# A fused attention and feed-forward kernel, its 1,400 operations put in another order up to the last stage

## The chip, the cores and the metric

The kernel runs on one core of a Trainium2 chip. The metric is the device time of one execution in microseconds (us), as the median of three runs. A core has TensorE (PE, matmuls), VectorE (DVE), ScalarE (ACT), GpSimd (POOL) and SyncE (SP). Each engine works through its own instructions strictly in order, and DMA transfers are issued from queues of POOL and SP.

## The reference, cut to what matters

```python
# q, k, v: (8, 12, 448, 64) float32
scores = (1 / sqrt(64)) * matmul(q, k.transpose(0, 1, 3, 2))
attn   = maximum(scores, 0) ** 2 / 448
x      = matmul(attn, v).transpose(0, 2, 1, 3).reshape(3584, 768)
h      = x @ w_in                                  # (768, 2048)
g      = 0.5 * h * (1 + erf(h / sqrt(2)))          # exact gelu
out    = g @ w_out                                 # (2048, 768) -> (3584, 768) float32
```

There is no softmax: the scores go through relu and a square, so each block of keys can be worked off by itself.

## The kernel before

**Tiling.** The work goes by batch (8), by group of four heads (3 groups, g0 to g2) and by block of 64 keys (7 blocks). Matmul operands are bf16.

**Into transposed form.** QK needs q and k with the head dimension on the partitions. Batches 0 and 1 are transposed on PE (`add_tk`, L607, for k; `add_tq`, L635, for q) and copied out of PSUM by DVE (L513) or ACT (L515). Batch 0 is worked in two halves of its 224 queries, so that the first half can begin when half of q is there. From batch 2 on, nine DMA transposes per batch on SP's queue do this (`add_T_dma`, L662): for each group one for k, one for its even and one for its odd q slots. The third kind reaches into the next group's q, so it waits for that load too.

**Attention.** QK (L736) writes score blocks into one of three double banks of PSUM ("w"). A relu takes them out, on ACT (L748) or on DVE (L750). A square on DVE (L757) makes the weights in place; there are 14 such buffers. AV (L797) sums a group over its blocks into a "w" bank, and a copy (L513 or L515) puts it into xT, two heads to 128 partitions.

**Feed-forward.** When all three groups of a half or of a batch are in xT, the first matmuls follow (`add_f1`, L849), 128 of the 2048 hidden columns at a time: `psh`, in one of two other PSUM banks ("f"), which the transposes of batches 0 and 1 use as well. ACT does the gelu (L859). Batch 0's first three tiles of hidden columns are computed by half rows (operations 141, 143 and 145 for the first half), so that PE has work before the second half of the queries is done; the first whole-row `psh` is operation 251. The second matmuls (`pso`, L1166) follow by groups of 256 rows; their sums and output copies are on DVE and ACT (L1147, L1200), three `osb` buffers hold results, and SP issues the stores (L1127; operations 386, 389, 435, 436 are the first). The last batches use sums over blocks of weights (L993, L1030, L1039, L1103) to save multiplications.

**Loads.** POOL's queue issues them: k (L548), q (L469), v (L566), `w_in` in five parts of three transfers (L486 to L488) and `w_out` in three (L492). Only the first group of batch 0 is loaded from other queues (L1312 to L1315). One buffer each holds the untransposed q and k of the DMA-transposed batches in turn, so before the loads of the next batch POOL runs a small copy, the "gate" (L703), that waits for the transposes of a group.

**Before the first data.** 45 matmuls on zeros (the "spin", L1333) run on PE. Later, "fills" (`add_fill`, L1493 to L1505) do the same in an "f" bank: a word Z1056 in the order is a fill of 1056 columns, in matmuls of at most 512 (L1499).

**What sets the order.** All operations are put in one list with their numbers. A constant, `ORDER` (L83 to L165), is a list of words that is written out in the code, each a letter for the engine (P for PE, A for ACT, D for DVE, G for POOL, S for SP, Z for a fill on PE) and an operation's number. `place` goes through it and gives each engine its instructions in that order:

```python
for word in ORDER.split():
    if word[0] == "Z":
        op, eng = next(fills), "PE"
    else:
        op, eng = self.open[int(word[1:])], names[word[0]]
    _, dur, lat = next(e for e in op.engines if e[0] == eng)
    ...
    self.commit(max(self.ready(op), free), op, eng, dur, lat)
```

So the list also says whether DVE or ACT does a relu or a copy. The waits between engines come from the operations' operands and buffers, not from the list.

The numbers that the text needs (b is the batch, g the group):

| operations | what they are |
|---|---|
| 0, 3 and 1, 4 | loads of k and of q's first half, b0 g1 and g2 |
| 2, 5, 6 | loads of v, b0 g0, g1, g2 |
| 7; 8, 9; 120, 124, 128 | load of q's second half, b0; `w_in` parts 0, 1; 2, 3, 4 |
| 117, 121, 125; 118, 122, 126; 119, 123, 127 | loads of b1: k, q, v of g0, g1, g2 |
| 147, 150, 153; 148, 151, 154; 149, 152, 155 | loads of b2: k, q, v |
| 228 to 236 | b2's transposes: k, even q, odd q of g0 (228, 229, 230), g1 (231 to 233), g2 (234 to 236) |
| 237, 240, 242; 238, 239, 241 | gates after b2's transposes; loads of `w_out` |
| 269 to 275; 398 to 406 | loads of b3; its transposes |
| 407, 410, 413; 408 to 416 without these; 541 to 549 | gates after b3's transposes; loads of b4; its transposes |
| 288, 306, 330; 440; 600, 624 | first QK in the list before: of b2 g0, g1, g2; of b3; of b4 g0 and g1 |
| 1435 | the identity matrix for PE's transposes (L1321) |

Of the kernel before, what the change touches and what calls it, by code (L numbers as in the profile page):

```python
# [80 lines left out]


ORDER = """  # L83
G0 G1 G2 G3 G1435 G4 G5 G6 A10 P11 D13 A16 P17 G7 D12 P14 D18 P42 P39 G8 P19 A15 P21 D43 P33 P36 D44
A40 D20 Z128 A22 P54 G9 P25 P23 A37 D34 P51 D26 P48 A55 Z1056 D35 A24 P69 D56 Z1024 D41 A49
P57 Z992 D38 A52 P63 Z448 G117 D70 P45 A58 D53 P66 A64 D50 P27 A46 G118 P31 D59 P60 D28 A67
G119 D32 A47 P78 P29 D65 G120 A61 P81 Z1088 D68 D30 A79 P93 D62 P108 Z544 D71 A82 P84 Z992
G121 A94 P75 D109 P72 G122 D83 A85 P90 P129 D80 G123 D73 A76 P105 A74 P102 D95 G124 P131 D130
A91 P141 D86 A106 D77 P111 P96 D132 A103 P165 P143 D92 A112 D104 D107 A97 P156 D113 P87 G125
D98 A166 P99 D110 G126 D88 A157 P114 A142 D100 A89 P174 G127 A101 P168 D115 P133 A144 P135  # L90
A116 G128 D175 P171 P159 A169 D134 P251 D136 D170 A160 P145 D158 A172 D167 A252 P162 P186 D176
P192 P243 A146 D161 G147 D173 A187 G148 P253 D193 A163 A244 D164 P195 G149 P180 P198 P137 A254
G150 P139 D196 A181 P183 P177 G151 D138 A199 D140 A184 P189 P219 P245 D178 G152 A190 D185 P247
G153 D194 A220 D179 A246 G154 P213 D188 P222 P204 P263 D221 A248 G155 D197 A214 D200 P265 D191
A205 D182 A264 P261 A223 A266 P216 D224 S231 P207 P201 D206 A262 A208 S229 P210 P259 D209 A217
D215 S232 P255 D211 A260 P249 D212 D218 A256 D202 P225 A203 S228 A250 P257 S230 A226 P267 D227
A258 P348 S234 A268 P350 S233 A349 P352 G237 A351 G238 P354 S235 A353 G239 P288 S236 P294 P282
P358 A355 G240 G241 D289 P356 D283 A359 P360 D295 A357 D290 P306 P279 P276 D296 P362 A361 D307
P364 D280 A363 P366 D277 A365 P368 A367 P370 A369 P300 P285 P291 G242 P372 A371 G269 D286 A292
P374 G270 D284 A373 G271 P318 P303 D301 P312 G272 P376 D308 A375 G273 A304 D319 P378 D278 A377  # L100
P380 D313 A379 D293 G274 D314 D390 P382 D305 G275 D302 A381 D391 D287 D281 P330 P309 P297 S398
D392 A331 D320 P315 S399 P384 D393 A298 D396 A310 S401 A383 D417 P387 D394 D419 A385 D311 A299
D395 A316 D317 P324 P321 D418 A325 P333 D397 P327 A388 P421 D420 D322 S400 A328 D323 P423 D326
A334 D422 S386 P339 P336 P342 P425 D424 D329 A343 D335 P427 S402 A426 D337 P429 G407 A340 G408
S403 D428 P431 G409 D344 D338 S389 D341 P440 P437 D332 P345 S404 D430 A438 P443 D441 P446 S405
P433 D432 A346 D347 A444 P509 A447 D434 P511 D439 G410 D448 S406 A510 G411 P449 D442 P452 G412
P455 P513 D562 A512 S435 D445 S436 A453 P515 D454 A450 A514 P517 D456 D451 P464 D457 P461 P458
S541 A465 P467 D462 A518 P470 G413 S542 P519 A516 G414 A459 G415 P521 D471 S543 G416 D472 A520
P523 D466 A468 D460 S544 A522 P479 D560 P476 P473 D469 P525 A524 D463 A477 P527 D480 A474 D478
A526 P529 D475 D481 A528 P488 P485 P482 S545 A489 P494 D486 A530 P491 P531 D487 D483 P533 D495  # L110
A532 S546 P535 D496 A484 D561 A492 P503 D490 P500 A534 P497 D493 P537 A536 G550 G551 S547 P564
D498 G552 A538 D504 S548 P539 D499 A501 G553 A565 D505 P600 G554 D502 P603 P506 G555 S549 A601
P606 D604 A540 P609 P566 D563 A507 D602 P568 D607 D567 P570 D610 A569 A508 P572 D571 P624 P612
P618 S704 P574 D580 D608 A613 D573 P576 S705 G556 A619 D581 G557 D582 P627 S706 D575 P615 G558
P584 D614 G559 D577 S578 A616 D611 P586 S707 D605 A628 D617 A625 P636 D620 P630 S579 A585 P621
D629 G713 A631 D637 P633 G714 P588 D587 S708 G715 A622 D626 D623 A634 P639 P642 P648 D583 P590
D638 A640 D635 A589 D632 P592 D641 A643 D591 P651 A649 S709 D644 P657 P645 D593 A652 P666 D658
P654 P594 D653 A646 D659 A655 D650 P596 A647 D667 S710 D595 P660 P766 P663 P672 D597 A661 D767
P674 A664 S711 D662 A673 D656 P676 D668 A675 D665 P772 P769 P669 S712 G716 D773 A770 P763 S598
P775 A677 G717 P678 S599 D670 G718 A764 D771 P680 G719 D723 A776 S867 D768 A679 P790 P778 D765  # L120
A671 P781 G720 P682 A681 D777 G721 D791 P684 G722 S868 D725 A683 P686 D779 A782 A685 P688 D783
D780 D774 P787 P793 P784 D724 S869 A788 P799 D794 A687 P796 P690 A689 D795 D789 A797 P692 D798
A691 P694 A693 P696 A785 A695 S870 P698 A786 A800 P802 P811 A697 P805 D801 P700 A699 A803 D812
P702 S871 D792 A806 D804 P814 P817 D807 P808 A815 S872 P823 D818 A701 P820 P727 G876 D816 A703
G877 D809 S873 A821 G878 D726 P729 A810 D819 A728 D822 P826 D813 A824 P829 S874 P906 P731 D730
G879 A830 G880 D827 S875 P733 G881 A907 D828 D831 P912 D825 P921 P832 D745 A913 P909 A732 D922
P924 P735 D734 A833 A925 P737 A910 D743 A834 P936 D914 P918 P933 D736 P739 D738 S741 D744 A934
P747 D908 G882 A937 D740 G883 P749 D938 A919 S978 G884 D935 A748 G885 D926 P942 P930 S742 P915
P751 D750 A931 D943 S979 P753 D920 A916 A752 D746 P755 D923 S980 D911 D944 P948 P945 D917 P927
D888 A949 D754 P939 P757 D950 A928 D886 D756 P759 A946 D887 A940 D758 A929 P835 D932 D947 D941  # L130
S981 P957 P954 P951 A836 D958 A955 P960 P963 D760 P837 D959 A961 D952 P839 D956 A953 S982 A838
P966 D964 P972 P969 D962 P841 A840 S983 D889 A973 D965 P843 S984 A842 D967 P847 A970 S985 A844
P845 D971 D968 S761 D974 P990 P987 D1067 P975 S986 A991 P993 D988 A846 P996 S762 P849 D992
A848 D1068 A976 D1070 P851 A997 D989 A850 P853 A994 A977 D995 P1005 P1002 A852 P999 P855 A854
D1006 A1003 P859 D1004 A1000 D998 A856 P857 D1007 D1001 P1011 P1014 P1008 D1059 A858 A1012
P1017 D1015 P1026 P861 A1009 D1063 A860 P863 D1060 A1018 D1010 P1020 A1027 P1029 D1061 P1023
A862 P865 D1016 A864 D1019 P890 A1021 D1028 D1022 A866 P892 D1062 A1024 A891 D1013 P894 D1025
A1030 D1069 D893 P1035 D1031 P1038 P1032 D1064 A895 A1036 D1066 P1041 D1037 A1039 P1044 P896
D1033 A1042 D1034 D1040 P898 A1045 D1043 D897 P1047 D1046 P1050 P1053 P900 D899 A1048 D1139
P902 D1049 A1051 D1140 A1054 P1071 D1052 D1055 P1056 D901 S904 A1072 D903 S905 P1088 D1141  # L140
P1073 D1057 P1090 A1089 D1058 P1143 D1074 D1091 P1075 D1065 P1092 A1144 P1077 D1142 A1076
D1179 P1094 A1093 D1180 P1079 D1078 P1096 D1095 P1145 D1080 D1097 A1081 P1082 D1181 A1098
P1099 D1146 P1085 D1083 P1102 D1100 A1084 P1105 D1086 A1101 P1122 D1103 A1087 P1107 D1182
A1106 P1124 A1123 P1147 A1104 D1108 D1125 P1109 P1126 A1148 P1111 A1110 P1128 A1127 P1113
D1112 P1130 D1129 P1149 D1114 D1131 A1115 P1116 A1132 P1133 D1150 P1119 D1117 P1136 D1134
A1118 P1151 D1120 A1135 D1137 A1121 P1153 D1291 A1138 D1292 D1152 P1155 D1159 D1154 S1157
P1163 D1160 D1156 S1158 P1165 D1161 D1164 P1167 D1162 D1166 D1293 P1169 D1294 A1168 P1171
D1170 P1173 D1253 D1172 P1175 D1251 D1174 S1177 P1183 D1252 P1200 D1176 S1178 P1185 A1184
D1254 P1202 A1201 P1255 D1186 D1203 P1187 P1204 A1256 P1189 A1188 P1206 A1205 P1191 D1190
P1208 D1207 P1257 D1192 D1209 A1193 P1194 A1210 P1211 D1258 P1197 D1195 P1214 D1212 A1196  # L150
P1217 D1198 A1213 P1234 D1215 A1199 P1219 A1218 P1236 A1235 P1259 A1216 D1220 D1237 P1221
P1238 A1260 P1223 A1222 P1240 A1239 P1225 D1224 P1242 D1241 P1261 D1226 D1243 A1227 P1228
A1244 P1245 D1262 P1231 D1229 P1248 D1246 A1230 P1263 D1232 A1247 D1249 A1233 P1265 A1250
D1264 P1267 D1271 D1266 S1269 P1275 D1272 D1268 S1270 P1277 D1273 D1276 P1279 D1274 D1278
P1281 D1280 P1283 D1282 P1285 D1365 D1284 P1287 D1363 D1286 S1289 P1295 D1364 P1312 D1288
S1290 P1297 A1296 D1366 P1314 A1313 P1367 D1298 D1315 P1299 P1316 A1368 P1301 A1300 P1318
A1317 P1303 D1302 P1320 D1319 P1369 D1304 D1321 A1305 P1306 A1322 P1323 D1370 P1309 D1307
P1326 D1324 A1308 P1329 D1310 A1325 P1346 D1327 A1311 P1331 A1330 P1348 A1347 P1371 A1328
D1332 D1349 P1333 P1350 A1372 P1335 A1334 P1352 A1351 P1337 D1336 P1354 D1353 P1373 D1338
D1355 A1339 P1340 A1356 P1357 D1374 P1343 D1341 P1360 D1358 A1342 P1375 D1344 A1359 D1361  # L160
A1345 P1377 A1362 D1376 P1379 D1383 D1378 S1381 P1387 D1384 D1380 S1382 P1389 D1385 D1388
P1391 D1386 D1390 P1393 D1392 P1395 D1394 P1397 D1405 D1396 P1399 D1403 D1398 S1401 P1407
D1404 D1400 S1402 P1409 D1406 D1408 P1411 D1410 P1413 D1412 S1423 P1415 D1414 P1417 D1416
P1419 D1418 S1424 P1420 D1421 S1425 D1422 S1426
"""  # L165


# [1368 lines left out]
```

## Time and profile before

| | |
|---|---|
| median of 3 runs | 370.13 us (369.83 to 370.37) |
| the profiled execution: its span (the page gives no other time of it) | 367.9 us, 8474 instructions |
| busy: PE, DVE, ACT, POOL | 359.3, 285.1, 199.4, 62.9 us |
| share of the span | 98%, 78%, 54%, 17% |
| read from memory, written to it | 45.61 MB, 11.01 MB |

How to read it: the span goes from the first to the last recorded instruction of one profiled execution, and is 2.2 us below the median of the runs. Busy times are sums over an engine's instructions; an engine can be busy and do nothing useful, as PE is with spin and fills. The view by stretches of time cuts the span into pieces and gives for each the busy time of every engine, the granted clock of PE and the share of the DMA engines. The view in order of time lists single instructions with start, length and, in brackets, the wait just before and what ended it; an entry "SPq" or "POOLq" is the issue of a DMA on that engine's queue, which takes time on the queue and lands later.

### The profile page before, as it was taken

What the parts mean: (1) busy time and instruction counts of PE and PEld (TensorE: products, weight loads), DVE (VectorE), ACT (ScalarE), POOL (GpSimd) and SP (SyncE); (2) the same over time, 40 slices, a digit from 0 to 9 for tenths busy, and PEclk for the clock granted to TensorE, in tenths of its full rate; (3) what the DMA queues carried; (4) which work ended last, traced back from release to release, by engine and by line L of the source; (5) the groups of instructions that cost most, each with busy time, mean ns of one, the idle gap of its engine ahead of it and who ended that gap; (6) DMA issues with size and microseconds to landing.
All of it is one profiled execution on the core that took longest, in us unless ns stands there. A gap on an engine that the chain in (4) does not pass through costs nothing.

```text
span 367.9 us, 8474 instructions
## 1 busy us (share of the span) xinstructions
PE 359.3 (98%) x3573; PEld 222.5 (60%) x3573; DVE 285.1 (78%) x473; ACT 199.4 (54%) x319; POOL 62.9 (17%) x103
## 2 busy tenths in 40 slices
PE   7999999999999999999999999999999999999995
PEld 6675654455544455544555544557876897688663
DVE  4998854699788889989598997998788558665862
ACT  5998954536367546765777568863540353045200
POOL 8766304230112140240302000000000000000000
PEclk9999999999999999999999999999999999999998
DMA  9999999999999999999999980002002301210233
GB/s 180 191 202 204 201 178 167 196 201 178 162 218 214 154 186 193 237 214 154 166 110 131 215 183 2 2 2 86 3 0 87 88 0 52 86 37 2 86 87 86
DMA packets 89542, 47.27 MB, mean 128 GB/s; under 512 B 55329, under 2 KB 86049, under 8 KB 89505
## 3 DMA queue, kind: packets, MB, share of 16 engines
q0 software_dynamic: 32912, 22.47, 43.8%
q1 hardware_dynamic: 55952, 23.76, 34.9%
q8 instruction: 28, 0.46, 0.5%
q10 hardware_dynamic: 640, 0.51, 0.4%
q14 instruction: 10, 0.07, 0.1%
HBM read 45.61 MB, written 11.01 MB: 154 GB/s over the span
## 4 chain that ended last, share of the span: by engine, by line
PE 78%; DMA 8%; SPq 5%; DVE 5%; issue 1%; POOL 1%; ACT 1%; DVEq 0%; POOLq 0%; ACTq 0%
PE pso L1166 30%; PE psh L849 19%; PE pb L993 13%; PE ps L736 8%; PE pav L797 7%; SPq L662 5%; DMA wout_sb<-in_moe_w_out_dram 4%; DVE a_sq L757 2%; DMA nq<-in_q_dram 1%; DVE t_sb L1103 1%; DMA qT<-nq 1%; DMA out_dram<-osb 1%; ACT a_sq L748 1%; PE tp L635 1%; DVE part L1030 1%
## 5 line engine op out<-in xcount | busy, mean ns | idle before, releaser
L748 ACT ACTIVATE a_sq<-ps 128x896 bf16<-128x896 f32 (+1 forms) x119 | 104.3, 918 | 36.8 <-PE ps L736 36.6
L757 DVE TENSOR_TENSOR a_sq<-a_sq 128x896 bf16<-128x896 bf16 (+1 forms) x169 | 97.0, 617 | 9.4 <-ACT a_sq L748 8.8
L849 PE MATMUL psh<-xT,win_sb 128*128 128x448 bf16 (+1 forms) x516 | 96.4, 340 | 0.4 <-issue 0.4
L849 PEld LDWEIGHTS <-win_sb 128*128 128x128 bf16 x516 | 48.1, 98 | 45.8 <-issue 9.7
L750 DVE TENSOR_SCALAR a_sq<-ps 128x896 bf16<-128x896 f32 (+1 forms) x50 | 53.5, 1078 | 17.1 <-PE ps L736 17.0
L859 ACT ACTIVATE h_sb<-psh 128x448 bf16<-128x448 f32 x80 | 43.2, 548 | 29.9 <-PE psh L849 29.6
L1166 PEld LDWEIGHTS <-s_sb 128*128 128x128 bf16 x424 | 40.7, 98 | 26.6 <-issue 2.0
L1030 DVE TENSOR_TENSOR part<-pb,part 128x448 f32<-128x448 f32 x60 | 34.6, 620 | 21.5 <-PE pb L993 21.5
L736 PE MATMUL ps<-qT,kT 64*64 64x448 bf16 (+1 forms) x756 | 47.9, 336 | 0.5 <-ACT a_sq L748 0.2
L1166 PEld LDWEIGHTS <-h_sb 128*128 128x128 bf16 x312 | 29.6, 98 | 22.5 <-issue 4.4
L1166 PE MATMUL pso<-wout_sb,s_sb 128*128 128x384 bf16 (+2 forms) x216 | 38.1, 320 | 0.1
L1166 PE MATMUL pso<-wout_sb,h_sb 128*128 128x384 bf16 x208 | 38.1, 326 | 0.0
L1166 PE MATMUL pso<-t_sb,s_sb 128*128 128x384 bf16 x208 | 38.1, 326 | 0.0
L797 PE MATMUL pav<-a_sq,v_sb 64*64 64x448 bf16 (+1 forms) x756 | 36.5, 329 | 0.3 <-issue 0.2
L736 PEld LDWEIGHTS <-kT 64*64 64x64 bf16 x756 | 18.5, 105 | 22.9 <-issue 17.1
L1039 ACT ACTIVATE h_sb<-part 128x448 bf16<-128x448 f32 x36 | 20.1, 578 | 20.2 <-DVE part L1030 19.9
L1200 DVE TENSOR_TENSOR osb<-pso,p_sb 128x384 f32<-128x384 f32 x39 | 21.7, 556 | 11.0 <-PE pso L1166 6.7
L993 PEld LDWEIGHTS <-win_sb 128*128 128x128 bf16 x288 | 27.6, 98 | 2.3 <-issue 0.4
L797 PEld LDWEIGHTS <-v_sb 64*64 64x64 bf16 x756 | 21.2, 107 | 11.7 <-issue 1.3
L703 POOL COPY gate<-qT 128x16 bf16<-128x16 bf16 x15 | 3.7, 246 | 111.0 <-DMA qT<-nq 111.0
L993 PEld LDWEIGHTS <-ws 128*128 128x128 bf16 x216 | 20.7, 98 | 0.0
L1147 DVE TENSOR_TENSOR s_sb<-h_sb 128x1024 bf16<-128x1024 bf16 x26 | 17.8, 685 | 2.3 <-PE pso L1166 2.3
(61 smaller groups left out, 298.4 us busy)
## 6 DMA issues: line engine op xcount, KB each, us to landing
nk<-in_k_dram POOLq DMA_DIRECT2D x23, 224.0 KB, 5.6
nq<-in_q_dram POOLq DMA_DIRECT2D x21, 224.0 KB, 8.3
v_sb<-in_v_dram POOLq DMA_DIRECT2D x5, 672.0 KB, 13.9
out_dram<-osb SPq DMA_DIRECT2D x8, 336.0 KB, 2.9
v_sb<-in_v_dram POOLq DMA_DIRECT2D x9, 224.0 KB, 8.6
out_dram<-osb SPq DMA_DIRECT2D x7, 288.0 KB, 3.2
out_dram<-osb SPq DMA_DIRECT2D x8, 240.0 KB, 3.0
win_sb<-in_moe_w_in_dram POOLq DMA_DIRECT2D x8, 192.0 KB, 8.6
```

The source lines that it names most:

```text
L736: nc.tensor.matmul(ps[64 * j : 64 * j + 64, e, x * w : x * w + w], kT[r, g, i * 128 + 64 * j : i * 128 + 64 * j + 64], moving, start=True, ...
L748: A.activation(ar, ps, AF.Relu, scale=c_att)
L750: V.tensor_scalar(ar, ps, c_att, 0.0, op0=mybir.AluOpType.mult, op1=mybir.AluOpType.max,)
L757: V.tensor_mul(box["a2"][:, :, :used], ar, ar)
L797: nc.tensor.matmul(pav[0][o2 : o2 + 64, e, :w], vt[b][r, 2 * g + e, bass.ts(i, D)], box["a2"][r, y, o : o + w], start=(i == 0), stop=(i == ...
L849: nc.tensor.matmul(ph[:, x * n : x * n + n], win_sb[:, kd, bass.ts(m + x, 128)], xT[b][:, kd, c], start=(kd == 0), stop=(kd == KD - 1),)
L859: A.activation(h_ring()[:, m : m + nm, o + c.start : o + c.stop], box[0][:, :S].rearrange("p (x n) -> p x n", x=nm), AF.Gelu,)
L993: nc.tensor.matmul(bank[name][:, y, z * HS : z * HS + HS], w[:, k, bass.ts(mm, 128)], right()[:, k], start=first and k == 0 and z == 0, st ...
L1030: V.tensor_add(get(to), ps(name), get(other))
L1039: A.activation(h_ring()[:, m : m + 2, o + half[c].start : o + half[c].stop], src().rearrange("p (x n) -> p x n", x=2), AF.Gelu,)
L1166: nc.tensor.matmul(box[bank][:, n0:n1], left()[:, kf], right()[:, kf, n0:n1], start=bool(need) and kf == 0, stop=kf == K2 - 1, skip_group_ ...
L1200: V.tensor_add(out()[:, n0:n1], box[bank][:, n0:n1], other()[:, n0:n1])
```

## The change

Only `ORDER` changes: it is replaced from its second line to the middle of its last stage; the last 164 operations stand as before. All operations, their operands and their buffers are the same, but for the fills: seven of eight go (Z128, Z1024, Z992, Z448, Z1088, Z544, Z992), and Z1056 stays. With seven fewer, the identity's number is 1428 instead of 1435. Lines below the list shift by two.

The opening, to the first whole-row `psh` (P251):

```diff
-G0 G1 G2 G3 G1435 G4 G5 G6 A10 P11 D13 A16 P17 G7 D12 P14 D18 P42 P39 G8 P19 A15 P21 D43 P33 P36 D44
-A40 D20 Z128 A22 P54 G9 P25 P23 A37 D34 P51 D26 P48 A55 Z1056 D35 A24 P69 D56 Z1024 D41 A49
-P57 Z992 D38 A52 P63 Z448 G117 D70 P45 A58 D53 P66 A64 D50 P27 A46 G118 P31 D59 P60 D28 A67
-G119 D32 A47 P78 P29 D65 G120 A61 P81 Z1088 D68 D30 A79 P93 D62 P108 Z544 D71 A82 P84 Z992
-G121 A94 P75 D109 P72 G122 D83 A85 P90 P129 D80 G123 D73 A76 P105 A74 P102 D95 G124 P131 D130
-A91 P141 D86 A106 D77 P111 P96 D132 A103 P165 P143 D92 A112 D104 D107 A97 P156 D113 P87 G125
-D98 A166 P99 D110 G126 D88 A157 P114 A142 D100 A89 P174 G127 A101 P168 D115 P133 A144 P135
-A116 G128 D175 P171 P159 A169 D134 P251
...
+G0 G1 G3 G1428 G4 G7 G118 A10 P11 D13 G2 A16 P17 D12 P14 G117 D18 P42 P39 G5 P19 D15 P36 D43
+G121 P21 A40 P33 D20 G6 P23 D44 A37 D22 P54 G8 P51 D41 P25 A34 D24 Z1056 D26 A55 P63 P57 D35 A52
+P31 P66 D64 P27 A58 D32 P108 P48 D38 P29 A67 D28 P81 P131 A109 G9 D49 P69 P45 A82 D56 P111 D50
+A70 P78 A46 D68 D47 A112 P75 P102 D53 A79 D30 P84 G122 P133 D59 A103 P60 D71 A85 G120 D65 P72
+D132 A76 D113 P93 A61 P129 A73 D80 D62 P90 D74 G125 P96 A94 P105 D130 P141 A91 D83 D110 A97 P165
+G124 P171 D134 P143 A142 D86 D95 A106 P168 D77 P135 A166 G126 D104 P87 D107 A172 P114 D98 A169
+D92 A88 P99 A115 D136 A89 P159 D116 P195 P145 G119 D167 A160 G128 A100 D196 P156 A144 D101 P174
+P162 A146 P137 P251
...
```

The words of the two DMA queues, each in its order. POOL's, to batch 4's last load (559 is a load of batch 5's v):

```diff
-0 1 2 3 1435 4 5 6 7 8 9 117 118 119 120 121 122 123 124 125 126 127 128 147 148 149 150 151
-152 153 154 155 237 238 239 240 241 242 269 270 271 272 273 274 275 407 408 409 410 411 412
-413 414 415 416
+0 1 3 1428 4 7 118 2 117 5 121 6 8 9 122 120 125 124 126 119 128 148 147 154 127 151 150 123
+237 238 239 149 153 241 240 272 152 242 271 270 155 269 274 273 407 408 275 413 409 410 414
+415 416 412 559 411
```

SP's, to batch 4's transposes:

```diff
-231 229 232 228 230 234 233 235 236 398 399 401 400 386 402 403 389 404 405 406 435 436 541
-542 543 544 545 546 547 548 549
+229 228 230 232 233 231 236 235 234 402 400 399 398 403 405 401 404 386 406 541 543 548 542
+549 435 547 545 389 546 436 544
```

The first QK of a group stand earlier among PE's words: those of batch 2's group 0 stand behind 39.9 us of PE's other work instead of 52.8, added up from the durations in the trace before. DVE gets 19 more operations (489 for 470) and ACT 19 fewer (298 for 317): 36 relus go from ACT to DVE and 32 the other way, the rest are copies and output sums.

## The prediction

> **What bounds the kernel now.** I read the page first, then stretches of 10 us, then the rows of the first 30 us and of the two DMA queues.
>
> ```profile
> span 367.9 us, 8474 instructions
> ...
> PE 359.3 (98%) x3573; PEld 222.5 (60%) x3573; DVE 285.1 (78%) x473; ACT 199.4 (54%) x319; POOL 62.9 (17%) x103
> ...
> PEclk9999999999999999999999999999999999999998
> ```
>
> PE is the bound, at the full clock. What can be won is time in which PE does nothing useful, and the stretches say where that lies:
>
> ```profile
> 0.00:10.00 10.00, 7.52 (x136) 6.29 (x138) 3.92 (x10) 6.03 (x9) 8.90 (x17) 1.00 1.02 183
> 10.00:20.00 10.00, 9.57 (x227) 6.45 (x225) 9.84 (x19) 9.35 (x14) 7.36 (x11) 1.00 1.45 190
> 20.00:30.00 10.00, 9.96 (x245) 7.67 (x242) 9.09 (x19) 8.92 (x16) 6.02 (x10) 1.00 1.28 205
> 30.00:40.00 10.00, 9.62 (x135) 6.24 (x135) 8.20 (x14) 8.37 (x12) 5.39 (x10) 1.00 1.27 202
> ```
>
> The columns are the stretch, its length, then PE, PEld, DVE, ACT, POOL, clock, DMA share, GB/s. From 10 to 20 DVE (9.84) and ACT (9.35) are full; PE's 9.57 holds the zero fills. So in the opening PE waits for relus, squares and copies. After 30 us only small PE waits are left: 0.38 in 30 to 40, 0.53 in 96 to 104, 0.18 at 241, 0.07 at 271.
>
> ```profile
> 9.72 0.39 PE L635 MATMUL tp<-ident,nq 112*64 112x112 bf16 x8 [0.86 <-DMA nq<-in_q_dram]
> ...
> 10.16 0.39 DVE L513 COPY qT<-tp 128x448 bf16<-128x448 bf16 x1 [0.75 <-PE tp L635]
> ...
> 10.55 0.91 ACT L515 COPY kT<-tp 128x896 bf16<-128x896 bf16 x1 [0.56 <-PE tp L607]
> ...
> 10.84 0.61 PE L1499 MATMUL fill<-zero 64*64 64x512 bf16 x3
> ```
>
> Group 2's q lands at 9.68, behind a v; PE, DVE and ACT all wait for it.
>
> **The change, part by part.** The span is the profiled execution's own 367.9; the median of the runs is 370.13, 2.2 above it, and I take that 2.2 as unchanged.
>
> *Fills.* 13 of 16 zero matmuls go. They lie between 8.46 and 18.99 and fill waits, so alone they save nothing. They cover the clock: it stays 1.00 through the 0.86 gap, and the spin's matmuls go from 107 to 56 ns apart after 2.8 us of work. Without the fills I find no gap over 1 us, so I price them at 0; were the clock lost, PE's first 2.8 us of full rows would take twice as long, up to 1.4.
> [...]
>
> *k and q ahead of v.* Landings of before: k g1 6.02, q g1 6.66, v 7.76, k g2 9.05, q g2 9.68. Taking out the v (1.1) puts q g2 at 8.6. The v loads then land at about 12.5, 14.8 and 17.1 (from 7.76, 10.84 and 12.69), and the new order asks for them at 13.9, 17.6 and 18.4: hidden. win goes from 16.5 and 18.5 to 19.1 and 21.1 and is asked for at 20.9 and 22.5: hidden by 1.4 or more.
>
> *Squares by need; who does what.* I count DVE's work up to the last half-row xT copy, which frees the first whole-row psh (op 251, L849). Steps, start to start: relu 1.00 (0.54 for a single block), square 0.535 (0.306), copies 0.30 (448 columns), 0.533 (896), xT 0.307. Before: 3 relus and 0.54, 20 squares and 2 small, 5 small and 3 large copies, 5 xT, and 0.73 for the cast and kT's 384 columns: 20.2. It runs from 4.73 to 28.32, so 3.4 are lost, 2.6 of them idle rows. After: the same 3 relus, 21 squares, 6 small and 6 large copies, 5 xT, 0.35 for kT's 512 columns: 23.0. Placing the first 20 operations by their inputs leaves only 0.9 of waits (0.47 for the first transpose, 0.3 to 0.4 for the next two, small ones), as DVE now has copies and squares where it waited. So it ends at 4.73 + 23.0 + 0.9 = 28.65. PE then needs one QK (its buffer is freed by this copy) and one transpose group (0.4), and starts op 251 at 29.35, against 29.91. By then it also has more behind it: psh 145 (1.20), two QK (0.43) and k transposes 137 (0.42). In PE steps, the new order has 20.1 us of work behind it at op 251; before gets there at 31.9. **Gain of the opening: 31.9 - 29.35 = 2.5.** With twice the waits it is 1.6, with none 3.4.
>
> *Work moved from ACT to DVE.* DVE has 19 more instructions (489 for 470), ACT 19 fewer: net 4 relus, 4 xT copies, 7 osb additions and copies, some 10 us in 240. DVE idles 83 us in all; from 140 to 160 it is full (9.73 and 10.00 of 10), yet PE waits nowhere there. I take 0; where the cover is gone, a relu is 0.19 slower than on ACT, at most 0.5 in all.
>
> *The loads of batches 2 to 4.* Here the new order takes something back. It calls QK of batch 2 much sooner. In PE work: first QK of batch 2 group 0 after 39.9 us of work (before gets there at 52.8, and itself starts that group at 60.0); group 1 after 44.2 (57.2; 64.2); batch 3 group 0 after 79.6 (93.1; 100.6); batch 4 group 0 after 108.4 (123.6; 131.1) and group 1 after 116.7 (132.1; 138.6). Each needs DMA transposes (L662). Where these land later than the first number in brackets, the gain is gone.
>
> ```profile
> 45.62 1.33 SPq L662 DMA_TRANSPOSE kT<-nk  x1
> 47.06 4.98 SPq L662 DMA_TRANSPOSE qT<-nq  x2
> 52.09 1.29 SPq L662 DMA_TRANSPOSE kT<-nk  x1
> 53.43 2.17 SPq L662 DMA_TRANSPOSE qT<-nq  x1
> ...
> 57.18 4.60 SPq L662 DMA_TRANSPOSE qT<-nq  x3
> ```
> ```profile
> 57.91 0.20 POOL L703 COPY gate<-qT 128x16 bf16<-128x16 bf16 x1 [14.95 <-DMA qT<-nq]
> 58.37 2.68 POOL L492 DMA_DIRECT2D wout_sb<-in_moe_w_out_dram  x3 [0.25 <-issue]
> ```
> ```profile
> DMA to landing us min/median/max: 3.3/6.4/10.9
> ```
>
> A transpose hardly moves while loads are queued: the last load of batch 2 lands at 51.75, the first three transposes (issued 45.6, 47.1, 48.8) at 52.5, 53.3 and 55.5, the rest about 1.3 apart. Those of the last row, issued with the wout loads, take 7.2 and 10.9; the one issued 1.2 ahead of them takes 3.3.
> [...]
>
> Group 0: the loads up to q of group 1 are as many as before's up to 44.84; two more at 1.15 to 1.3 end at 47.4. The third transpose then lands at 47.4 + 3.5 = 50.9. PE, at a gain of 2.5, wants it at 50.3. That leaves 1.9 at most.
> Group 1: its last transpose (k, op 231) is now the sixth and is issued when the third has landed, at 51.1; the gate (L703) waits for the same third one, and the first wout load follows at 51.6. So op 231 is issued 0.5 ahead of wout, between the row of 3.3 (1.2 ahead) and that of 7.2 (0.1 behind): it lands between 54.4 and 58.3. I take the middle, 56.3, as 0.5 lies midway. PE at the full gain wants it at 54.7; before reaches that work at 57.2. **What is left: 57.2 - 56.3 = 0.9.**
> Later, with the same spacings: batch 2 group 2 at 78.5 (k is now loaded behind 5.6 MB of wout's source) for 79.6; batch 3 group 0 at 91.8 for 93.1; batch 4 group 0 at 122 for 123.6; its group 1, whose last transpose now stands behind three stores on SP, at 131.8 for 132.1. Each leaves 0.3 to 1.6, and all are uncertain by 1.5 or so. These are ceilings on one gain, not costs that add up.
> The waits of before in 96 to 104 (0.53, for osb and its stores) may stay or go; stores 386 and 389 are now later on SP, each holding one of three osb buffers. I take them as they are, between a gain of 0.5 and a loss of 0.5.
>
> Sum: 370.13 - 0.9 = 369.2.
>
> **Rivals.**
> 1. *The forecast*: opening gains 2.5, the transposes give back 1.6: 369.2. For it: the row of 7.2. Chance 0.33, by itself 368.5 to 370.
> 2. *The transposes keep up*: op 231 goes like the row of 3.3 and lands by 54.7. The whole 2.5 stays, with part of the 0.53: 367.4. For it: T1 and T2 are issued 5 to 7 us ahead of the last load, and the profile shows slack of 2.2 or more at every later batch. Against it: each batch is now called some 7 us sooner. Chance 0.23.
> 3. *The transposes starve* (slower): op 231 falls wholly behind wout. At 7.2 from issue it lands at 58.3, PE stands 1.1 later than before: 371.2; at 10.9 it is 62.0 and 374.9. It decides from a landing after 57.2. The same can come later, at batch 4 group 1 after 132.1. Chance 0.33.
> 4. *The opening doesn't gain*: DVE and ACT are full from 10 to 20, and relus and squares are the same number; if the waits stay 3.4, op 251 starts at 31.85, where before has the same work done: 370.1. Against it: the waits have named causes that go. Chance 0.11.
>
> **How the numbers follow.** A run of this kernel can tell about 0.2% (0.74 us) from no change. Faster by more: 0.23 of rival 2, 0.20 of the forecast, 0.01 of rival 4: 0.44. Within: 0.10 of the forecast, 0.02 of rival 3, 0.06 of rival 4: 0.18. Slower: 0.03, 0.31, 0.04: 0.38. The range goes from 366.7 (2.95 of the opening, midway between 2.5 and 3.4, and 0.5 gained) to 372.2 (rival 3 at 7.2, with DVE's 0.5 and the osb waits' 0.5 lost): what is left out is most of rival 3's longer case and gains beyond.
>
> **What would show it.** Right: q g2 lands before 9; ACT goes from relu to relu from 7 us on; op 251 starts by 29.5; PE has a wait of 0.5 to 2 on ps (L736) near 51 or 55, put down to qT or kT; the clock stays 1.00. Wrong: a PE wait over 2.5 there or near 120 to 135 (rival 3); none at all (rival 2); DVE rows idle for PE below 25 us (rival 4); a clock of 0.5 before 30.

## The result and the profile after

The changed kernel takes 378.76 us (median of 6 runs, 378.42 to 382.75), before 369.98 (6 runs): ratio 1.0248, 95% interval 1.0217 to 1.0279, 9 us **slower**. The forecast was 369.2 with a range to 372.2. Run again later, beside before on one chip, it took 381.13 (4 runs) for 370.16 (1.0271, 1.0182 to 1.036). The profiled execution shown here is the longest of the first six (382.75); the one of the later run (381.16, span 379.3) is close to its median and serves as the measure for the experiments. In the times below, two single runs that were over 1.5% longer than the fastest of their kernel count as slow and are left out, 384.26 with v late and 377.28 with the later stages alone.

From the page of the changed kernel:

```profile
span 381.0 us, 8452 instructions
...
PE 363.4 (95%) x3560; PEld 224.0 (59%) x3560; DVE 295.9 (78%) x492; ACT 187.8 (49%) x300; POOL 64.2 (17%) x103
...
PEclk9999998999969999999999999999999999999999
```

PE is busy for 4 us more although 13 zero matmuls are gone, and the clock, full up to the last slice in before, has an 8 and a 6 in it. Its waits (engine, line, what it waited for: us in all, times, the longest):

```profile
PE pav L795 <- DVE a_sq L755: 4.7, 1, 4.7
PE ps L734 <- DMA kT<-nk: 3.7, 2, 3.0
PE pb L991 <- DVE part L1028: 1.3, 2, 0.7
```

And the stretches where before had 9.5 or more of 10 everywhere (columns as in the prediction):

```profile
10.00:20.00 10.00, 8.19 (x233) 5.98 (x232) 9.99 (x20) 9.81 (x15) 5.36 (x8) 1.00 1.34 199
...
50.00:60.00 10.00, 7.04 (x96) 3.33 (x94) 3.69 (x7) 5.09 (x9) 6.89 (x10) 0.99 1.13 154
60.00:70.00 10.00, 10.00 (x61) 4.37 (x60) 5.37 (x8) 5.77 (x9) 0.91 (x2) 0.84 1.29 193
...
100.00:110.00 10.00, 5.29 (x47) 2.88 (x49) 3.86 (x7) 3.02 (x4) 1.19 (x3) 0.88 1.06 168
110.00:120.00 10.00, 10.00 (x72) 4.76 (x65) 8.23 (x14) 3.08 (x5) 4.59 (x7) 0.78 1.15 166
```

After the opening two stretches have PE idle, and each is followed by one in which PE is "busy" for all of 10 us at a clock of 0.84 and 0.78: the same matmuls, some at half speed (twelve `psh` take 4.13 from 59.78, the clock at 0.50 for most of it; twelve in before, from 71.39 at 1.00, take 2.44).

To see where the time goes I use a running **lead**: add up the columns of all matmuls that PE has started (spin and fills left out; a matmul on a half or a quarter of the 128x128 of `psh` counts half or a quarter, as QK and AV with their 64x64: in before twelve QK of 448 columns take 0.76 us and twelve `psh` of 448 columns 2.44), and look up when before had done as many. Plus is ahead of before, in us; each row is one profiled execution, good to some 0.2:

| at (us) | 55 | 70 | 90 | 120 | 190 | 300 |
|---|---|---|---|---|---|---|
| changed kernel, shown above | 1.2 | -3.8 | -4.2 | -10.9 | -11.3 | -13.2 |
| changed kernel, later run | 1.3 | -1.7 | -3.2 | -9.0 | -9.2 | -11.4 |

So the opening gains 1 and holds it to 55; 3 to 5 are lost from 59 to 70, 0.4 to 1.5 between 70 and 90, 6 to 7 between 100 and 120, some 2 between 210 and 290.

### The profile page after: what moved, and what is told of

Same layout as the page of the kernel before. It is cut to its first block, busy times and chain, and to the rows that moved or that the text cites. A ratio compares the mean times of both kernels' runs of the same rounds, so it can differ in the third digit from the quotient of the medians.

```text
span 381.0 us, 8452 instructions
## 1 busy us (share of the span) xinstructions
PE 363.4 (95%) x3560; PEld 224.0 (59%) x3560; DVE 295.9 (78%) x492; ACT 187.8 (49%) x300; POOL 64.2 (17%) x103
## 5 line engine op out<-in xcount | busy, mean ns | idle before, releaser
L746 ACT ACTIVATE a_sq<-ps 128x896 bf16<-128x896 f32 (+1 forms) x115 | 100.9, 920 | 52.0 <-PE ps L734 51.8
L847 PE MATMUL psh<-xT,win_sb 128*128 128x448 bf16 (+1 forms) x516 | 97.8, 344 | 0.0
L847 PEld LDWEIGHTS <-win_sb 128*128 128x128 bf16 x516 | 48.5, 99 | 46.5 <-issue 11.1
L748 DVE TENSOR_SCALAR a_sq<-ps 128x896 bf16<-128x896 f32 (+1 forms) x54 | 58.1, 1077 | 22.8 <-PE ps L734 22.3
L1164 PEld LDWEIGHTS <-h_sb 128*128 128x128 bf16 x312 | 30.2, 99 | 21.5 <-issue 4.1
L795 PE MATMUL pav<-a_sq,v_sb 64*64 64x448 bf16 (+1 forms) x756 | 37.8, 336 | 5.3 <-DVE a_sq L755 4.7
L795 PEld LDWEIGHTS <-v_sb 64*64 64x64 bf16 x756 | 21.5, 108 | 17.1 <-issue 6.5
L701 POOL COPY gate<-qT 128x16 bf16<-128x16 bf16 x15 | 5.0, 337 | 98.8 <-DMA qT<-nq 87.2
L1164 PE MATMUL pso<-t_sb,h_sb 128*128 128x384 bf16 x104 | 20.1, 339 | 0.0
```

The lines of the kernel that those rows point to most:

```text
L746: A.activation(ar, ps, AF.Relu, scale=c_att)
L748: V.tensor_scalar(ar, ps, c_att, 0.0, op0=mybir.AluOpType.mult, op1=mybir.AluOpType.max,)
L795: nc.tensor.matmul(pav[0][o2 : o2 + 64, e, :w], vt[b][r, 2 * g + e, bass.ts(i, D)], box["a2"][r, y, o : o + w], start=(i == 0), stop=(i == ...
L847: nc.tensor.matmul(ph[:, x * n : x * n + n], win_sb[:, kd, bass.ts(m + x, 128)], xT[b][:, kd, c], start=(kd == 0), stop=(kd == KD - 1),)
L1164: nc.tensor.matmul(box[bank][:, n0:n1], left()[:, kf], right()[:, kf, n0:n1], start=bool(need) and kf == 0, stop=kf == K2 - 1, skip_group_ ...
```

## The experiments

### The opening: four runs on one chip

New order up to P251, then before's words (the loads in between too):

```diff
-G0 G1 G2 G3 G1435 ... P251 (before)
+G0 G1 G3 G1428 G4 ... P251 (changed), then before's words without these
```

> The new order up to P251 (the loads of POOL that stand there included), then the words of before in their order (three words changed places by one, so that a PSUM bank is free). Theory A (the loss lies in two later stalls): the opening keeps the 1.0 us by which the changed kernel is ahead at 50 us, and no stall over 1 us follows, as batch 2's transposes are issued as in before with 2.2 of slack: 369.98 - 1.0 = 369.0. Rival (the new opening itself feeds the stalls, by calling everything sooner): a wait of over 1 us on kT or qT near 60, no gain or slower, 370 to 373. What would also count against A: 367.5 or less, that is the 2.5 that was forecast.

Measured: 370.23 beside 370.12, ratio 0.9997 (0.9975 to 1.0019). The lead is 0.6 at 15, 0.3 at 30, and -2 at 50: the join makes PE wait 0.7 for k's transposes and 0.7 for a gelu. No wait over 1 follows, but the join costs more than the opening gains, so this run settles nothing about what would be kept.

Only the fills out:

```diff
-Z128 Z1056 Z1024 Z992 Z448 Z1088 Z544 Z992
+Z1056
```

> Before without seven of its eight fills, nothing else. Theory: the fills only lie in waits and the clock needs none of them: 369.98, no difference over 0.3, clock 1.00 to 365. Rival 1 (the clock is lost in the opening without them): a clock of 0.5 for some us before 30, 371.4 or so. Rival 2 (a fill sometimes stands in the way of a real matmul): 0.3 to 0.6 faster.

370.05, ratio 0.999 (0.9969 to 1.0012), the clock 1.00 in the opening: the fills cost and bring nothing, as forecast.

Only POOL's first loads in another order:

```diff
-G0 G1 G2 G3 G1435 G4 G5 G6 ... G7
+G0 G1 G3 G1435 G4 G7 G2 G5 ... G6
```

> Before with POOL's first loads in another order: 0 1 3, identity, 4 7, then the v loads 2 5 6; all else as before. Theory: q of g2 lands at 9.1 or a little sooner, the wait of 0.86 goes to 0.3, and 0.3 to 0.5 of it is left at the end: 369.5. Rival 1: DVE and ACT are the limit from there to 25 us anyway: 370.0. Rival 2: the first AV now waits for v, which lands at about 12 to 17: slower, 370.5 or more.

370.22, ratio 1.0001 (0.998 to 1.0022). q of g2 lands at 8.7 and the wait of 0.86 is gone, but the lead is 0.3 at 20 and 0.2 at 300: what lands next (k and q of batch 1 at 20.3 and 21.5) arrives in the very moment it is asked for.

The new work of the opening with before's order of loads:

```diff
 (words of the first run, POOL's among them as in before)
-G0 G1 G3 G1428 G4 G7 G118 G2 G117 G5 G121
+G0 G1 G2 G3 G1428 G4 G5 G6 G7 G8 G9
```

> Like the run with the new opening alone, but POOL's loads all in the order of before (nine words changed places by one). Theory: the new order of squares and of batch 1's transposes wants q's second half at 11.2, which then lands at 14.4, so the gain of 1.0 is lost and more: 371 to 372. Rival (the order of the squares brings the gain by itself): 369.0 to 369.5.

378.37, ratio 1.0221 (1.0185 to 1.0256), far more than expected:

```profile
PE tp L632 <- DMA nq<-in_q_dram: 7.1, 2, 4.2
```

PE waits 2.9 and 4.2 for q's second half and for q of batch 1, the granted clock is 0.50 from 15.6 to 25.9, and PE is 8.3 behind at 25. So **the new order of work needs the new order of loads**, which alone brought nothing. In the changed kernel, too, steps start soon after their loads land: q's second half 0.2, q of batch 1 0.8, k of batch 1 group 1 0.5, v of g2 0.4. But DVE is full there as well (9.99 of 10 from 10 to 20), and no run separates which of the two sets the pace. What remains on PE are small waits in between:

```profile
11.23 0.24 PEld L633 LDWEIGHTS <-nq 112*64 112x64 bf16 x8 [0.17 <-DMA nq<-in_q_dram]
...
15.73 0.39 PE L734 MATMUL ps<-qT,kT 64*64 64x224 bf16 x8 [0.29 <-ACT a_sq L746]
...
19.31 1.11 PE L795 MATMUL pav<-a_sq,v_sb 64*64 64x224 bf16 x37 [0.59 <-issue]
```

The last of these stands in the middle of a group's AV, and the profile finds nothing that it waits for.

### How far the new order may run

New order to D182, just ahead of batch 2's first transpose, then before's words:

```diff
 ... G123 A246 D182 (changed kernel)
-S229 P207 D179 ...
+(before's words from here)
```

> The new order up to D182, just ahead of the first DMA transpose of batch 2 (S229, 40.5 us in the changed kernel), and from there the words of before. Theory A (the loss is made by the transposes and loads after this point, the opening gains 1.0): the QK of batch 2 come at 60 again, k of group 1 (231) is issued first, no stall over 0.5 behind 40 us: 369.98 - 1.0 = 369.0. Rival (what the opening gains is gone at the end in any case, as loads land later or DVE and ACT owe work): 370.0 or more. If a stall over 2 us stands at 50 to 60 even here, A is wrong.

369.89 beside 369.95, ratio 1.0 (0.9989 to 1.0012). The lead is 1.3 at 30 and 1.8 at 41, in this profile more than in the changed kernel's, but 1.0 goes at 43 to a relu on DVE and 1.0 at 100:

```profile
PE pso L1163 <- DVE osb L1197: 1.4, 1, 1.4
...
PE ps L733 <- DVE a_sq L747: 1.0, 1, 1.0
```

The wait on `osb` stands in before too, with 0.4, and with 1.1 in the run with only the fills out. It is for store 386, which frees one of three buffers.

New order to S234:

```diff
 ... D284 S234 (changed kernel)
-D278 A373 P376 ...
+(before's words from here)
```

> The new order up to S234 (issued at 74.2 in the changed kernel), from there the words of before. It holds the first stall (59 us, on k of group 1) and not the second (104 to 109 us). Theory A (two separate stalls): PE is behind by 3.8 at 70 and stays there: 369.98 + 3.8 = 373.8, up to 375 if the join waits. Rival (the first stall is the cause of the second, which delays what follows from it): 377 or more, with a wait of over 3 us near 105.

372.99, ratio 1.009 (1.0061 to 1.0119), near the expected 373.8, but not for its reason: in this profile there is no wait at 59. PE waits 1.2 for k of group 2 (234) at 83.6 and 2.6 for an `osb` buffer at 103. So the loss near 104 does not need the one at 59.

### The wait at 59: a race between two issues

k of batch 2 group 1 first among the transposes:

```diff
-S229 P207 ... S228 ... S230 ... S232 ... S233 ... S231
+S231 S229 P207 ... S228 ... S230 ... S232 ... S233 ...
```

> The changed kernel with one word moved: S231 (k of batch 2 group 1) is the first transpose instead of the sixth, as in before. Theory A (231 is late because it stands behind five others and starts beside w_out's load): 231 lands by 51, the wait of 3.0 at 59 and the 1.6 of half clock behind it go: 378.8 - 4.6 = 374.2. Rival 1 (whichever transpose is last before the w_out loads starves, now q of group 1, 233 at its place): still a wait of 2 to 3 on qT, 378 to 379. Rival 2 (the second stall grows by what the first gives back, as it hangs on a landing): 376 to 379.

382.79, ratio 1.0346 (1.0306 to 1.0387): theory A fell.

```profile
PE ps L733 <- DMA qT<-nq: 4.2, 1, 4.2
PE pav L794 <- DVE a_sq L754: 4.2, 1, 4.2
PE ps L733 <- DMA kT<-nk: 1.8, 1, 1.8
```

231 now needs k of group 1 before anything else can go, and that load lands at 48.5. Group 0's transposes land up to 56.3, and PE, which wants them at 52.3, waits for these instead.

The gate ahead of w_out:

```diff
-G237 D212 G238 D224 P288 G239 ... G149 ... G153 ... G241 ... G240
+G237 D212 G240 G238 D224 P288 G239 ... G149 ... G153 ... G241
```

> The changed kernel with one word moved: the gate of batch 2 group 1 (G240, which waits for that group's transposes, 231 among them) stands ahead of the first w_out load (G238). No load is then queued while 231 is on its way. Theory A (231 takes 8.1 us because w_out's load is issued beside it): 231 lands 3.3 after its issue, at 54.5, and PE's wait of 3.0 at 59 with the clock behind it (1.6) goes; w_out and the loads behind it come 3.5 later, so k of group 2 (234, which lands at 83.9 just in time) makes PE wait 3 to 5 near 80 instead: within 1.5 of the run of the changed kernel on this chip. Rival (231 is slow for another reason, its place on SP or its own size): it lands near 59 still, and everything behind is later: 3 us slower than the changed kernel.

380.21 beside the changed kernel's 381.13 on the same chip; against before 1.0264 (1.0191 to 1.0336). 231 lands 5.0 after its issue, at 56.0, and there is no wait at 59; PE waits 3.3 at 82.6 for 234. Within 1.5, as theory A had it; but in the run with v late, below, 231 lands at 56.0 and no wait stands at 59 either, with the gate in its old place.

Why 231 takes so long shows best where the same words ran with other luck. In the run to S234 the two issues and the landing are (SP's queue, POOL's queue, time from issue to landing of that transpose):

```profile
51.12 1.24 SPq L659 DMA_TRANSPOSE kT<-nk  x1
```
```profile
51.48 1.91 POOL L489 DMA_DIRECT2D wout_sb<-in_moe_w_out_dram  x2 [0.25 <-issue]
```
```profile
DMA to landing us min/median/max: 3.0/3.0/3.0
```

and in the changed kernel:

```profile
50.93 1.24 SPq L660 DMA_TRANSPOSE kT<-nk  x1
```
```profile
50.89 2.65 POOL L490 DMA_DIRECT2D wout_sb<-in_moe_w_out_dram  x3
```
```profile
DMA to landing us min/median/max: 8.1/8.1/8.1
```

Issued 0.4 ahead of w_out's load it takes 3.0, issued 0.04 behind it 8.1. In the other runs with this stretch, 231 issued 1.2 and 2.5 ahead of the next load takes 5.0 each, and 0.04 to 0.1 behind it 7.2 to 7.6 (four runs). One run does not fit: 0.4 ahead, with the load of k of group 2 as the next one, it takes 7.1. So the order of the two issues goes with the landing in eight runs of nine, and what decides is not shown. The load is let go by the landing of 230, through the gate (in the changed kernel its wait of 11.38 ends with that); 231's issue follows that of 233 on SP (there at 50.93 and 49.54). Both chains start from the issue of 230, and either can come first.

### The wait at 104: a store behind a load, and DVE in order

On the changed kernel, in order of time:

```profile
107.95 0.56 DVE L1198 TENSOR_TENSOR osb<-pso,p_sb 128x384 f32<-128x384 f32 x1 [6.14 <-DMA out_dram<-osb]
108.43 0.61 DVE L755 TENSOR_TENSOR a_sq<-a_sq 128x896 bf16<-128x896 bf16 x1
...
109.09 2.45 PE L795 MATMUL pav<-a_sq,v_sb 64*64 64x448 bf16 x23 [4.71 <-DVE a_sq L755]
```

DVE waits 6.1 with an output copy for a free `osb` buffer; the square that PE needs stands behind it. The square first:

```diff
-D428 A447 P437 D338
+A447 P437 D338 D428
```

> The changed kernel with one word moved: on DVE the square D338, which AV of batch 2 group 2 (P345) needs, stands ahead of the output copy D428, which waits 6.1 us for a free osb buffer. Theory A (PE's 4.7 at 104 is DVE held up in order by a copy that PE does not need yet): the wait of 4.7 and the 2.0 of half clock behind it go: 378.8 - 6.7 = 372.1; D428 still waits for store 386, which still lands near 108. Rival (PE then waits for the PSUM bank that D428 empties, or for the relu D438 behind it): 2 to 4 us come back, 374 to 377.

380.84, ratio 1.0304 (1.0273 to 1.0334): theory A fell, and none of the rival's 2 to 4 us came back either. Its mechanism shows: the wait on the square is gone, and PE waits for the relu behind the same copy:

```profile
PE ps L733 <- DVE a_sq L747: 4.8, 2, 3.8
```

Batch 3's v late, out of the store's way:

```diff
-G275 P440 ... G415 D434 G416
+P440 ... G415 G275 D434 G416
```

> The changed kernel with one word moved: the load of batch 3's v (G275, 0.67 MB, not needed before 122) is issued behind G415 near 111 instead of at 96. Theory A (the store 386 takes 10.1 us to land because this load is issued 1.7 ahead of it): 386 lands by 103, DVE's wait of 6.1 for the osb buffer and PE's 4.7 near 104 go, with 2.0 of half clock: 6 us faster than the changed kernel on this chip. Rival 1 (the transposes around the store on SP hold it): 386 lands at 106 or later, no change. Rival 2 (another wait stands close behind, as when the square was put first): 2 to 4 faster.

379.29 (three runs, 377.35 to 380.33) beside the changed kernel's 381.13 (379.02 to 382.3), so the time by itself decides little. The trace does. Issue to landing of the store's two transfers, in the changed kernel and here:

```profile
DMA to landing us min/median/max: 9.5/9.7/9.9
```
```profile
DMA to landing us min/median/max: 3.6/3.8/4.0
```

The store lands in time, no wait stands at 104, and PE's only long one is

```profile
PE ps L733 <- DMA kT<-nk: 3.8, 1, 3.8
```

at 83, for 234. This profile is 4 ahead of the changed kernel's at 120. Of theory A the landing and the waits came as told, of its 6 us some 4, by the lead.

### The half clock

> The changed kernel itself, unchanged, as the run that the next three are held against on the same chip. Expected: 378.4 to 380; waits of PE of 3 on k of batch 2 group 1 near 59 and of 4.7 on the square near 104, each with some us of half clock behind it.

381.13 (1.0271, 1.0182 to 1.036), waits of 2.6, 1.6 and 4.4 at 59, 83 and 108; half clock around the last one alone (0.50 for 6.8 us).

Fills where PE waits (in a QK bank):

```diff
+Z7168 P318
...
+Z11264 P345
```

> The changed kernel with two fills of zeros where PE waits longest: 7168 columns (3.0 us) ahead of P318 and 11264 columns (4.7 us) ahead of P345, in a QK bank of PSUM. No wait is taken away. Theory A (behind each wait the clock is halved because PE stood idle, and that costs 1.6 and 2.0): the clock stays 1.00 and the kernel is 3.6 us faster than the changed kernel on this chip. Rival 1 (the clock falls for another reason): 0.5 for some us behind both, no change. Rival 2 (the fills themselves delay what follows): 1 to 3 slower.

382.93; against before 1.0338 (1.0243 to 1.0433). The clock holds:

```profile
59.00:67.00 8.00, 7.75 (x66) 3.37 (x65) 4.25 (x5) 5.32 (x8) 0.23 (x1) 1.00 1.28 188
...
108.00:116.00 8.00, 8.00 (x71) 4.00 (x61) 8.00 (x14) 3.02 (x5) 5.57 (x9) 1.00 0.91 129
```

and PE is 1.9 better off at 120 than the changed kernel on this chip, but at 250 both stand at -10.1. Keeping the clock did save time, and it was waited for again.

### What is behind each wait

The times of these runs (379.3 to 382.9) are no wider apart than those of the changed kernel itself (378.4 to 382.8), so this part is read from the profiles, one for each. In all but one a wait that is taken away comes back. The exception is the run with v late: of the 4.1 by which it is better off at 120 than the changed kernel's later run, 3.7 are left at 300. The leads (us, as above):

| at (us) | 55 | 70 | 90 | 120 | 190 | 300 |
|---|---|---|---|---|---|---|
| k of group 1 first | -2.2 | -5.6 | -7.0 | -11.9 | -12.8 | -15.0 |
| square first | 1.3 | -3.6 | -4.2 | -9.0 | -9.2 | -11.9 |
| gate first | 0.4 | 0.2 | -5.8 | -9.4 | -9.3 | -12.5 |
| v late | 0.4 | 0.2 | -5.8 | -4.9 | -5.1 | -7.7 |
| fills at the waits | 1.3 | -2.4 | -3.3 | -7.0 | -7.9 | -11.3 |
| k of group 2 early | 0.8 | -0.7 | -0.6 | -9.4 | -9.5 | -12.7 |
| k of group 2 early, v late | 1.7 | -2.0 | -1.9 | -3.2 | -9.9 | -12.5 |

The last two: the load of k of batch 2 group 2 ahead of w_out,

```diff
-G237 D212 G238 D224 P288 G239 ... G149 D203 ... P267 G153
+G237 G153 D212 G238 D224 P288 G239 ... G149 D203 ... P267
```

> The changed kernel with one word moved: the load of k of batch 2 group 2 (G153) stands directly behind the first gate, ahead of the w_out loads instead of behind two of them and v. Theory A (k of group 2 is the ceiling behind the first wait: its transpose 234 lands at 82.6 to 86.4 in all runs with this order of loads, and PE waits 0.7 to 3.8 there): 234 lands before 75, no wait near 84; what remains are the wait near 59 (0 to 3, as 231 is issued within 0.5 of the next load) and the one near 104 with its half clock: 376 to 378. Rival 1 (all comes back at the second wait near 104, as that hangs on a load's landing): 379 to 381. Rival 2 (the load in front of 231 makes the wait at 59 longer): a wait of 4 or more there, 380 or more.

382.51, ratio 1.031 (1.0268 to 1.0352). 234 lands at 71.0 and no wait is left at 84, as theory A had it; PE comes to 104 sooner and waits 7.1 there instead of 4.4: rival 1 by its cause, at more than its 381. And with v late as well:

```diff
-G275 P440 ... G415 D434 G416
+P440 ... G415 G275 D434 G416
```

> The run before with one more word moved: batch 3's v (G275) late, behind G415. Theory A (three waits, each a transfer that is behind loads queued ahead of need): no wait over 1 near 84 and near 104; left are 0 to 4.6 at 59 and some 3 behind 190, less 1 gained in the opening: 372 to 376. Rival (a further wait stands behind each): 378 or more.

381.45, ratio 1.0264 (1.0215 to 1.0314): the rival. It is 5.7 ahead of the changed kernel at 120 and has nothing of it at 190: PE waits 2.6 at 138 for k of batch 4 group 1 (544), which stands behind three stores on SP, and 2.0 at 174 (the profile names a square there, which QK does not read; a q transpose of batch 5 group 1, 709, lands 0.1 before PE goes on), with half clock behind it (0.50 for 3.4 us):

```profile
170.00:175.00 5.00, 3.03 (x23) 1.20 (x22) 4.89 (x8) 2.36 (x4) 0.56 (x2) 0.95 0.92 196
175.00:180.00 5.00, 5.00 (x20) 2.29 (x19) 2.52 (x4) 1.09 (x2) 4.31 (x7) 0.70 0.97 155
```

Why 709 is late is on SP's queue of the changed kernel:

```profile
154.66 2.85 SPq L660 DMA_TRANSPOSE qT<-nq  x2
168.43 0.79 SPq L1125 DMA_DIRECT2D out_dram<-osb  x2
169.74 1.46 SPq L660 DMA_TRANSPOSE kT<-nk  x1
171.25 1.29 SPq L660 DMA_TRANSPOSE qT<-nq  x1
```

SP stands for 11 us with a store whose rows are not computed yet, and two transposes are behind it; in before 709 was issued at 149.0. There is no time of a kernel with the new work and before's whole queues, or of the reverse, so the share of the queues' order against the earlier calls stays open.

### The later stages, and the stores

Before's words to P906 (187 us), then the new order:

```diff
 ... P906 (before)
-P731 D730 G879 ...
+(the changed kernel's words that are left)
```

> The words of before up to P906 (187 us), behind it the new order. Theory A (the waits of PE on the running sums near 278 and 290, 0.7 and 0.5, and what is lost around 220 to 250, are of the new order itself): 2 to 2.7 slower than before: 372 to 372.7, with the same two waits on pb. Rival (they follow from the delays before): 370.0.

371.90 (nine runs) beside 370.32, ratio 1.0056 (1.0029 to 1.0084): 1.6 slower by the medians, 2.1 by the ratio, so about theory A. The two waits on the block sums (0.72 and 0.55) stand here as in the changed kernel:

```profile
PE pb L991 <- DVE part L1028: 1.3, 2, 0.7
```

The new opening to D182, and the first two stores forward on SP:

```diff
-S398 ... S399 ... S401 ... S400 ... S386 ... S402 S403 ... S389
+S398 ... S399 ... S386 S401 ... S400 S389 ... S402 S403
```

> The new order up to D182 and the words of before behind it, as in the run until 47, and the first two stores moved forward on SP (386 ahead of transpose 401, 389 behind 400). Theory A (the opening's gain of 1.3 to 2 is waited for again at 99, where an output copy needs the osb buffer that store 386 holds, and this store stands behind transposes on SP): 386 is issued by 88 instead of 94.7, the wait of 1.4 on pso near 99 goes, and 0.5 to 1.5 of gain is left: 368.5 to 369.5. Rival (loads and other engines set the pace all the same): 369.8 to 370.5.

369.78 beside 370.32, ratio 0.9981 (0.9958 to 1.0005). The wait of 1.4 on `osb` is gone, so the ceiling was there, but 1.0 is still lost at 44, the lead is about 0 at 120, and the time lies at the rival's edge. No version that was run is clearly faster than before.

## Why the prediction was wrong

The sum had two terms, and both failed. The opening was to gain 2.5 and gained 1.0. Then the transposes and a store were to leave 0.9 of it; they land later than the sum had them, and PE is 9 to 11 behind at 120.

- **Right**: the fills (0, both in time and clock); q of g2 sooner (9.1, for 8.6); the mechanism of the ceilings. Transposes that cannot land at the time of the earlier call were named as what would decide, with 231 beside w_out as the first. It lands at 54.2 to 59.5 in the runs that leave its place on SP, for 54.4 to 58.3 forecast. Rival 3, at 0.33, was the case that came, though at more places than one and with more than its 374.9.
- **The opening: "So it ends at 4.73 + 23.0 + 0.9 = 28.65".** The lead at 30 us is 1.0 in the changed kernel and 0.3 to 1.3 over the profiles with this opening. DVE's operations were counted rightly, but with steps that are too short. The same steps give before 20.2 us, and with its 2.6 of idle rows 22.8, where DVE took 23.6; the missing 0.8 is missing in the 23.0 again. With 23.8 of work and 1.5 of waits (for 0.9) the last of these copies ends at 30.1:

```profile
6.12 0.39 DVE L511 COPY qT<-tp 128x448 bf16<-128x448 bf16 x1 [0.93 <-PE tp L633]
...
29.70 0.38 DVE L511 CAST xT<-pav 128x224 bf16<-128x224 f32 x1
```

Op 251 starts at 31.35 instead of 29.35: 1.4 of it is DVE's, 0.6 more lie between the two. The v loads, called hidden at 12.5, 14.8 and 17.1, land at 13.6, 15.9 and 19.1, the last 0.7 behind the 18.4 at which it was to be asked for; no wait of PE in this profile is put down to it.

- **The ceilings: "Each leaves 0.3 to 1.6".** The rule behind them holds: right after such a wait the lead is the time at which before has done the same work, less the landing, within 0.1. The landings were mis-sized, by 3 to 6 us where there was a forecast ("before has the work at" is by the measure of the lead):

| wait on | before has the work at | landing forecast | landing measured | lead measured |
|---|---|---|---|---|
| 231 (changed kernel) | 57.1 | 56.3 | 59.0 | -2.0 |
| 234 (changed kernel) | 79.5 | 78.5 | 83.9 | -4.4 |
| 544 (k of group 2 early, v late) | 132.0 | 131.8 | 138.0 | -6.0 |
| 709 (the same run) | 166.1 | none, past batch 4 | 174.3 | -8.2 |

So they are not ceilings on one gain but losses, whatever the opening gains. 544 stands behind stores of rows that PE itself computes late, so part of its lateness follows from the waits before. (The 52.8 given with the change is a time of this kind, too: when before has done 39.9 us of work, not the work ahead of its own QK, which starts at 60.0.)

- **Batch 2 group 2, "at 78.5 for 79.6".** Its k lands at 74.2 behind w_out (4.7 MB of its source, by the sizes on the page, not 5.6), and its transpose, issued then, takes 9.7 beside batch 3's loads, where 78.5 left it 4.3 (3.3 in before):

```profile
DMA to landing us min/median/max: 9.7/9.7/9.7
```

It lands at 82.6 to 83.9 in all but one run with this order of loads (86.4). PE waits 0.7 to 3.8.

- **"The waits of before in 96 to 104 ... between a gain of 0.5 and a loss of 0.5".** The store that frees the buffer was taken as it was; in before its two transfers land 3.2 and 3.6 after their issue. With a v load issued 1.7 ahead of it, they take 9.5 and 9.9, and DVE, in order, holds a square and a relu: 4.4 to 4.7, and the half clock.
- **The clock.** It was priced for the opening alone. Behind the waits at 59 and 109 it costs 1.6 and some 1.9 more, by the lead from 60 to 70 and from 110 to 120.
- **The later stages** were taken at 0 from DVE's idle time; by themselves they cost 0.6%.

## What to carry to other kernels

When work is called sooner, follow every transfer that it needs to the end of the pipeline and compare its landing with the time at which the old kernel had done the same work, not only with the new time of use: one that lands later than that is a loss that no gain in front of it can pay (the four waits of the table left PE 2.0 to 8.2 us behind). A single wait that is removed tells little while the next supply is as late; keep a running lead against the old kernel, which shows at once where time comes back. On a queue that works in order, a store that is not ready must not stand ahead of a transposing load that PE will need (here SP stood for 11 us), nor, on an engine, an output copy that waits for a buffer ahead of squares and relus (here DVE stood for 6.1).

## What the runs showed of the hardware

- A DMA transpose that took 3.0 us in the run to S234 took 7.2 to 8.1 in four runs in which w_out's load had been issued 0.04 to 0.1 before it, and 9.1 to 10.2 beside a row of loads. A store's transfers went from 3.6 and 4.0 to 9.5 and 9.9 with a v load issued 1.7 before them. So beside loads they took 2.4 to 3.4 times as long (7.2 and 10.2 for 3.0); how the queues share the DMA engines is not shown.
- In or behind waits of PE of 1.9, 2.0, 2.5 and all longer than 2.7 us the clock was 0.50 for 3.4 or 6.8 us (10.2 around the two long waits of the run with the new work and the old loads), and not behind others of 1.1, 1.6, 1.8 and 2.6; at 2.65 it went either way. What decides is not shown.
